# Sliding-window attention with a soft mixture of experts: long q and k runs with 32x32 vector transposes, one span of keys per query tile, dilated heads by residue, experts on four array columns

## The chip, the core and the metric

The kernel runs on one core of one Trainium2 chip. The metric is the device time of one execution in microseconds (us), here always the median of several executions. A kernel that is compared was run on the same chip, in turn with the kernel before. Runs more than 1.5% above the fastest run of the same kernel count as slow and are left out of every ratio.

In the profile, PE is TensorE's matmuls, PEld its loads of stationary operands, DVE is VectorE, ACT is ScalarE and POOL is GpSimd. GpSimd issues all large loads and stores here. "GB/s" counts bytes as they land in the on-chip memory. The inputs are fp32 in HBM and land as fp16, so a landed rate of 207 GB/s reads about twice as much from HBM; the outputs land as fp32.

## The reference

There are two stages in series. Attention has batch 8, 8 heads, 576 positions and 64 elements per head. Heads 0-3 ("plain") look back over 32 positions; heads 4-7 ("dilated") look back over 128 positions but only at every fourth.

```
scores = q @ k.T / sqrt(64)
rel = pos_q - pos_k
plain: 0 <= rel < 32          dilated: 0 <= rel < 128 and rel % 4 == 0
x = softmax(where(mask, scores, -1e9)) @ v      # then heads side by side: [4608, 512]

logits = x @ phi                                # [4608, 32], 8 experts x 4 slots
d = softmax(logits, over rows); c = softmax(logits, over slots)
slot_in = d.T @ x                               # [32, 512]: needs ALL rows of x
slot_out[e] = relu(slot_in[e] @ w1[e]) @ w2[e]  # w1: 512x1024, w2: 1024x512, per expert
out = c @ slot_out                              # [4608, 512]
```

The experts can start only when attention is finished for all rows, and no output row exists before the last expert's second layer. So the time is a sum of three stages: attention, experts, output.

q and k are drawn with a standard deviation of 0.1. A scaled score is therefore about 0.01 in size, and the softmax is nearly uniform over the window. The comparison with the reference cannot see an error in the scores.

## The kernel before

Loads go through GpSimd's queue, in blocks of 128 positions. Every row that lands is 64 elements: 256 bytes are read, 128 bytes land. A memset of the column of ones (which gives the softmax sum as a 65th output) stands behind each v load.

```
def load_qk_blk(ti, b, blk):
    ...
    src = ten[b, :, s0 : s0 + ns, :].rearrange("h p d -> p h d")
    nc.gpsimd.dma_start(out=t[0:ns], in_=src)

def load_v_blk(b, kb):
    ...
    nc.gpsimd.dma_start(
        out=vt[0:nk, :, 0:D], in_=v[b, :, s0 : s0 + nk, :].rearrange("h p d -> p h d")
    )
    nc.gpsimd.memset(vt[0:nk, :, D : D + 1], 1.0)
```

TensorE transposes q and k, two heads at a time, and VectorE copies each result out of PSUM. Scores are then one matmul per head and key block, on 64 rows of the array.

```
# transposes of one tensor and one pair of heads: 5 matmuls, then one copy
nc.tensor.transpose(ring[:, blk, 0:ns], inp, ident16[0:ns, 0:ns])
...
nc.vector.tensor_copy(out=tt, in_=ring.rearrange("r b c -> r (b c)")[:, 0:S])
...
for h in range(2):                       # emit_scores
    p0 = 64 * h
    nc.tensor.matmul(sps[0:nk, h, 0:ncol], kT[p0 : p0 + 64, q0 : q0 + nk],
                     qT[p0 : p0 + 64, q0 : q0 + ncol], start=True, stop=True)
```

The experts run one after another. Each matmul has only the 4 slots of one expert as its stationary operand, and 512 moving columns.

```
for fc in range(2):                      # emit_expert_w1(e)
    hps = psum_h.tile([S_PER_E, 512], FP32, ...)
    for dc in range(4):
        nc.tensor.matmul(hps, siT[:, dc, 4 * e : 4 * e + 4],
                         w1t[:, dc, 512 * fc : 512 * fc + 512], ...)
...
for hc in range(FDIM // 128):            # emit_expert_w2(e)
    nc.tensor.matmul(sops, hT_sb[:, hc, :], w2t[:, hc, :], start=(hc == 0), stop=(hc == 7))
```

The loads of batch b+1 are issued while batch b computes. Five w1/w2 pairs are loaded during attention, the other three after it.

The softmax here doesn't subtract the row's maximum and nothing guards it: scores larger than these inputs give would overflow.

## Time and profile before

The time before was 291.85 us (median of 3, 287.37 to 293.52). One profiled execution had a span of 287.0 us.

| stage | from, to (us) | what limits it |
|---|---|---|
| attention, 8 batches | 0-213 | loads, with TensorE close behind |
| experts, 128 matmuls | 213-258 | matmuls in series, late weight loads |
| output, 9.4 MB | 260-287 | DMA, up to 407 GB/s |

These are lines of the page of the kernel before: busy time per engine, then the span in 40 equal slices (a digit is the busy share in tenths), the landed rate in each slice, and the count of DMA packets by size.

```profile
span 287.0 us, 4940 instructions
...
PE 243.9 (85%) x1786; PEld 123.8 (43%) x1786; DVE 142.9 (50%) x478; ACT 113.6 (40%) x318; POOL 139.9 (49%) x220
...
PE   5469799895899979987998799689996999969990
...
DMA  9999999999999999999999999900009999408999
GB/s 116 127 96 126 82 115 124 153 175 115 114 174 176 102 112 193 166 114 116 190 150 111 135 186 136 111 5 2 0 3 177 204 208 210 83 2 232 407 405 275
DMA packets 131208, 41.09 MB, mean 143 GB/s; under 512 B 114128, under 2 KB 122352, under 8 KB 131184
```

The DMA row stands at 9 up to the 26th slice (187 us), but the rate below it wanders between 82 and 193 GB/s, while the weights that are loaded late move at 204-210. 114,128 of the 131,208 packets are below 512 B. So the DMA engines are busy with short rows. TensorE is busy for 85% of the span.

The timeline of GpSimd in the kernel before shows the issues (start, duration, line, operation, and in brackets the idle time before it and what ended that):

```profile
56.06 0.88 POOL L134 DMA_DIRECT2D v_0_974<-in_v_dram  x1 [1.21 <-PE s_2_4_903 L200]
56.93 0.89 POOL L127 DMA_DIRECT2D qk_3_1_1015<-in_q_dram  x1
57.79 0.90 POOL L127 DMA_DIRECT2D qk_3_1_1017<-in_k_dram  x1
58.95 0.89 POOL L134 DMA_DIRECT2D v_1_1019<-in_v_dram  x1 [0.26 <-issue]
68.16 0.13 POOL L137 MEMSET v_0_974<- 128x8 f16 x1 [8.31 <-DMA v_0_974<-in_v_dram]
```

Each issue costs 0.9 us, and there are 15 per batch. The memset behind the load of v block 0 waits for that load to land, and everything behind it in GpSimd's queue waits too: 8.3 us here. The view of waits of the same kernel has one such line per batch:

```profile
POOL v_0_2177 L137 <- DMA v_0_2177<-in_v_dram: 10.0, 1, 10.0
POOL v_0_1375 L137 <- DMA v_0_1375<-in_v_dram: 9.6, 1, 9.6
```

The chain of waits that ended last confirms it. From 56 us on, its long pieces are (start, duration, piece):

```profile
56.06 12.05 DMA v_0_974<-in_v_dram
...
82.31 13.11 DMA v_0_1375<-in_v_dram
```

The two stand 26 us apart, which is the time of one batch. How close TensorE follows is seen in two windows of the kernel before: one batch in the middle, and the last batch, for which nothing is loaded any more. Columns: window, length, busy time of PE, PEld, DVE, ACT, POOL, granted clock, the time that DMA packets took as a share of the 16 engines' time (above 1 where they overlap), GB/s.

```profile
56.00:82.00 26.00, 21.41 (x202) 12.60 (x202) 16.03 (x61) 10.95 (x37) 14.39 (x22) 0.71 1.54 140
187.00:209.00 22.00, 21.21 (x160) 11.54 (x160) 13.48 (x45) 10.88 (x42) 0.13 (x1) 0.58 0.00 1
```

Without loads the last batch takes about 22 us instead of 26, with TensorE busy for 21.2 of them. So mending the loads alone could not give more than some 5 us per batch; TensorE's work has to shrink as well.

### The profile page before, as it was taken

How to read it: one execution, taken by the hardware profiler on the slowest of the kernel's cores; microseconds unless marked ns; L12 is line 12 of the kernel's file. 1: busy time of each engine (PE TensorE's matmuls, PEld its weight loads, DVE VectorE, ACT ScalarE, POOL GpSimd, SP SyncE). 2: the span in 40 equal slices, each digit the busy share in tenths (PEclk: the TensorE clock that was granted, in tenths of full speed). 3: DMA queues.
4: the chain of work that ended last, by engine and by line, in shares of the span. 5: the costliest groups of instructions: out<-in, count | busy, mean ns of one | idle time of the engine just before them, and what ended most of it. 6: DMA issues, size and time to landing. Idle time of an engine off the chain costs nothing.

```text
span 287.0 us, 4940 instructions
## 1 busy us (share of the span) xinstructions
PE 243.9 (85%) x1786; PEld 123.8 (43%) x1786; DVE 142.9 (50%) x478; ACT 113.6 (40%) x318; POOL 139.9 (49%) x220
## 2 busy tenths in 40 slices
PE   5469799895899979987998799689996999969990
PEld 1135455553446544554455446436552343322110
DVE  2038566867266764765466448636763000006662
ACT  1015443643434434362344235333713344426551
POOL 7888587634780658087419634600012110007993
PEclk9855555979555675595566557755789799995555
DMA  9999999999999999999999999900009999408999
GB/s 116 127 96 126 82 115 124 153 175 115 114 174 176 102 112 193 166 114 116 190 150 111 135 186 136 111 5 2 0 3 177 204 208 210 83 2 232 407 405 275
DMA packets 131208, 41.09 MB, mean 143 GB/s; under 512 B 114128, under 2 KB 122352, under 8 KB 131184
## 3 DMA queue, kind: packets, MB, share of 16 engines
q0 software_dynamic: 130304, 40.38, 125.4%
q1 hardware_dynamic: 880, 0.39, 0.7%
q8 instruction: 14, 0.23, 0.4%
q14 instruction: 10, 0.08, 0.1%
HBM read 62.23 MB, written 9.44 MB: 250 GB/s over the span
## 4 chain that ended last, share of the span: by engine, by line
DMA 41%; PE 29%; POOL 16%; issue 8%; ACT 2%; DVE 1%; POOLq 0%; ACTq 0%
POOL out_dram L575 5%; DMA v_0_2177<-in_v_dram 5%; DMA v_0_1375<-in_v_dram 5%; DMA v_0_974<-in_v_dram 4%; DMA v_0_2578<-in_v_dram 4%; DMA v_0_1776<-in_v_dram 4%; DMA v_2_208<-in_v_dram 2%; DMA v_2_2664<-in_v_dram 2%; DMA v_3_1913<-in_v_dram 2%; DMA v_3_1111<-in_v_dram 2%; DMA v_2_1461<-in_v_dram 2%; DMA v_0_159<-in_v_dram 2%; DMA v_3_180<-in_v_dram 2%; DMA v_0_194<-in_v_dram 2%; DMA qk_6_4_2349<-in_k_dram 2%
## 5 line engine op out<-in xcount | busy, mean ns | idle before, releaser
L575 POOL DMA_DIRECT2D out_dram<-outt_3702 x1 | 0.6, 561 | 28.2 <-ACT outt_3702 L564 28.2
L148 POOL DMA_DIRECT2D w_5_3378<-in_moe_w_dram x1 | 0.8, 766 | 25.9 <-PE o_2_4_3291 L256 25.9
L561 PEld LDWEIGHTS <-ET 32*128 32x128 f16 (+1 forms) x40 | 4.2, 116 | 19.7 <-issue 19.5
L388 PE MATMUL warm_136<-masks_sb 128*128 128x512 f16 x16 | 6.4, 591 | 3.4 <-DMA masks_sb<-masks_d 3.4
L510 PEld LDWEIGHTS <-siT 128*4 128x4 f16 x64 | 5.2, 90 | 8.4 <-issue 2.4
L350 PEld LDWEIGHTS <-E_row 128*32 128x32 f16 (+1 forms) x40 | 4.1, 114 | 9.8 <-issue 8.7
L310 PEld LDWEIGHTS <-phi_64 128*32 128x32 f16 x64 | 5.5, 109 | 5.4 <-issue 3.9
L213 ACT ACTIVATE praw_0_0_271<-s_0_0_257 128x318 f16<-128x318 f32 x1 | 0.4, 438 | 17.2 <-PE s_0_0_257 L200 17.2
L388 PEld LDWEIGHTS <-masks_sb 128*128 128x128 f16 x30 | 3.2, 121 | 7.8 <-issue 4.1
L256 PEld LDWEIGHTS <-ptm_76 128*128 128x128 f16 (+1 forms) x64 | 4.9, 113 | 3.6 <-issue 0.9
L173 DVE COPY qT_0_225<-ring_q_0_226 128x576 f16<-128x576 f16 x1 | 0.5, 458 | 11.7 <-PE ring_q_1_234 L169 11.7
L256 PEld LDWEIGHTS <-ptm_82 128*128 128x128 f16 (+1 forms) x64 | 5.0, 117 | 3.0 <-issue 0.6
L256 PEld LDWEIGHTS <-ptm_85 128*128 128x128 f16 (+1 forms) x64 | 5.5, 119 | 0.8
L256 PEld LDWEIGHTS <-ptm_79 128*128 128x128 f16 (+1 forms) x64 | 4.9, 118 | 1.5 <-issue 0.7
L330 PEld LDWEIGHTS <-ET 32*128 32x128 f16 (+1 forms) x40 | 3.7, 100 | 3.7 <-issue 1.2
L148 POOL DMA_DIRECT2D w_7_3423<-in_moe_w_dram x1 | 0.8, 759 | 8.8 <-PE hps_1_3417 L510 8.8
L137 POOL MEMSET v_0_2177<- 128x8 f16 x1 | 0.1, 133 | 10.0 <-DMA v_0_2177<-in_v_dram 10.0
L137 POOL MEMSET v_0_1375<- 128x8 f16 x1 | 0.1, 133 | 9.6 <-DMA v_0_1375<-in_v_dram 9.6
L256 PEld LDWEIGHTS <-ptm_83 128*128 128x128 f16 (+1 forms) x48 | 3.7, 118 | 2.4 <-DVE qT_1_832 L173 0.6
L256 PEld LDWEIGHTS <-ptm_77 128*128 128x128 f16 (+1 forms) x48 | 3.7, 117 | 2.3 <-issue 0.9
L256 PEld LDWEIGHTS <-ptm_80 128*128 128x128 f16 (+1 forms) x48 | 3.8, 117 | 1.3
L137 POOL MEMSET v_0_2578<- 128x8 f16 x1 | 0.1, 133 | 8.4 <-DMA v_0_2578<-in_v_dram 8.4
(2096 smaller groups left out, 879.8 us busy)
## 6 DMA issues: line engine op xcount, KB each, us to landing
w_0_860<-in_moe_w_dram POOLq DMA_DIRECT2D x1, 1024.0 KB, 8.3
w_0_862<-in_moe_w_dram POOLq DMA_DIRECT2D x1, 1024.0 KB, 12.9
w_1_1261<-in_moe_w_dram POOLq DMA_DIRECT2D x1, 1024.0 KB, 8.1
w_1_1263<-in_moe_w_dram POOLq DMA_DIRECT2D x1, 1024.0 KB, 11.9
w_2_1662<-in_moe_w_dram POOLq DMA_DIRECT2D x1, 1024.0 KB, 8.1
w_2_1664<-in_moe_w_dram POOLq DMA_DIRECT2D x1, 1024.0 KB, 11.5
w_3_2063<-in_moe_w_dram POOLq DMA_DIRECT2D x1, 1024.0 KB, 8.1
w_3_2065<-in_moe_w_dram POOLq DMA_DIRECT2D x1, 1024.0 KB, 13.3
```

What stands on the lines that cost most here:

```text
L137: nc.gpsimd.memset(vt[0:nk, :, D : D + 1], 1.0)
L148: nc.gpsimd.dma_start(out=w1t, in_=moe_w1[e].rearrange("(c p) f -> p c f", p=128))
L173: nc.vector.tensor_copy(out=tt, in_=ring.rearrange("r b c -> r (b c)")[:, 0:S])
L213: nc.scalar.activation(out=praw[0:nk, :, 0:ncol], in_=sps[0:nk, :, 0:ncol], func=AF.Exp, scale=SCALE)
L256: nc.tensor.matmul(opair[0:nq, col, :], lhs, rhs, start=(i_mm == 0), stop=(i_mm == len(mms) - 1),)
L310: nc.tensor.matmul(lp[:, 0:ncl], phi16[:, kc, :], xTb[:, kc, c0 : c0 + ncl], start=(kc == 0), stop=(kc == 3),)
L330: nc.tensor.transpose(erps[0:ns], ET_sb[:, r0 : r0 + ns], ident16[0:32, 0:32])
L350: nc.tensor.matmul(up, E_row[0:ns, blk, :], xb[0:ns, t, :], start=(iu == 0), stop=(iu == NQB - 1),)
L388: nc.tensor.matmul(wps, lhs, rhs, start=True, stop=True)
L510: nc.tensor.matmul(hps, siT[:, dc, 4 * e : 4 * e + 4], w1t[:, dc, 512 * fc : 512 * fc + 512], start=(dc == 0), stop=(dc == 3),)
L561: nc.tensor.matmul(fp[0:ns], ET_sb[:, r0 : r0 + ns], so_sb, start=True, stop=True)
L575: nc.gpsimd.dma_start(out=out[r0 : r0 + ns, :], in_=ot[0:ns])
```

## The change

Four things are rewritten at once. The intent is to make rows long and take transposes off TensorE, to cut the matmul columns that the mask throws away, and to run four experts side by side.

1. **Loads.** One q or k load brings 4 heads x 576 positions as 128 partitions of 18 positions each: runs of 4608 bytes read, 2304 landed. Dilated v comes in runs of four positions and is spread by GpSimd. Plain v still comes in 64-element rows, in six loads of 96 positions, each with its four heads. The columns of ones are written once, at the start.
2. **Transposes.** VectorE transposes q and k in 32x32 blocks of 4-byte words (two fp16 each), 6 instructions per batch.
3. **Scores.** A plain query tile of 96 positions meets one span of 128 keys. Dilated heads are sorted by position modulo 4, so that each residue is an ordinary window of 32. Scores contract over 32 rows twice.
4. **Experts.** Four experts write to four 32-column groups of the array.

The diff, cut to its core ("..." marks cuts):

```diff
-        src = ten[b, :, s0 : s0 + ns, :].rearrange("h p d -> p h d")
-        nc.gpsimd.dma_start(out=t[0:ns], in_=src)
...
+            nc.gpsimd.dma_start(
+                out=t, in_=ten[b].rearrange("(g h) (p j) d -> (h p) g (j d)", g=2, j=PJ)
+            )
...
+    def load_v_plain(b):
+        vt = vP[b % NV]
+        for t in range(NT):
+            nc.gpsimd.dma_start(
+                out=vt[32:128, t, :, 0:D],
+                in_=v[b, 0:4, QT * t : QT * t + QT, :].rearrange("h a d -> a h d"),
+            )
...
+        nc.gpsimd.dma_start(
+            out=sa, in_=v[b, 4:8, 0:512, :].rearrange("h (a r) d -> a h (r d)", r=DIL)
+        )
+        nc.gpsimd.dma_start(
+            out=sb[0:48], in_=v[b, 4:8, 384:576, :].rearrange("h (a r) d -> a h (r d)", r=DIL)
+        )
...
-            nc.vector.tensor_copy(out=tt, in_=ring.rearrange("r b c -> r (b c)")[:, 0:S])
+        src = raw[(ti, b)][:, 0, :].bitcast(U32).rearrange("p (j m) -> p j m", m=32)
+        t = qTp[b % 2] if ti == 0 else kTp[b % 2][:, 32 : 32 + S, :]
+        dst = t.rearrange("p s t -> p (s t)").bitcast(U32).rearrange("p (a j) -> p j a", j=PJ)
+        nc.vector.transpose(out=dst, in_=src)
...
+        for kt_, k0, qt_, q0, c0, w in jobs:
+            for tt in range(2):
+                for hh in range(2):
+                    p0 = 32 * (2 * pair + hh)
+                    nc.tensor.matmul(
+                        sps[:, hh, c0 : c0 + w],
+                        kt_[p0 : p0 + 32, k0 : k0 + 128, tt],
+                        qt_[p0 : p0 + 32, q0 : q0 + w, tt],
+                        start=(tt == 0),
+                        stop=(tt == 1),
+                    )
...
+            if att and kt == 1:
+                if b + 2 < B:
+                    load_qk(0, b + 2)
+                    load_qk(1, b + 2)
+                    load_w1(b)
...
+            if att and kt == 3 and b + 2 < B:
+                load_v_plain(b + 2)
+                load_v_dil(b + 2)
...
+    for fc in range(2):
+        for g in range(2):
+            for dc in range(4):
+                for j in range(4):
+                    e = 4 * g + j
+                    nc.tensor.matmul(
+                        hps[32 * j : 32 * j + 32, fc, :],
+                        siTm[:, dc, e, :],
+                        w1t[e][:, dc, 512 * fc : 512 * fc + 512],
...
+    jobs = [(0, c, j) for c in range(8) for j in range(4)]
+    jobs += [(1, c, j) for j in range(4) for c in range(8)]
+    for g, c, j in jobs:
+        nc.tensor.matmul(
+            so[32 * j : 32 * j + 32, :],
...
```

## The prediction

> **What bounds the kernel now.** Three stages in series (table of windows).
> Attention, 0-213 us. The 40-slice view shows the DMA engines at 9 tenths from 0 to 187 us but only 82-193 GB/s landed (fp16, half of what is read), while the late weight loads land 204-210. 114,128 of 131,208 packets are under 512 B (queue line): q, k and v come as 256-byte rows. The chain of waits between 56 and 187 us is mostly loads of 11-13 us with GpSimd issues of 0.9 us each; a memset behind each v load makes the GpSimd queue wait 8-10 us per batch (view of waits). A batch takes 26 us. TensorE is close behind: once everything has landed (187-209 us) the last batch still takes about 21 us, at a granted clock of 0.5-0.8, about 110 ns for each of its 190 matmuls.
> Experts, 213-258 us: 128 matmuls of 512 columns with 4 stationary columns, about 240 ns apart, in series.
> Output, 258-287 us: 9.4 MB at up to 407 GB/s, DMA-bound.
>
> **What the change does.**
> 1. q and k rows become 2304-byte landed runs, half of v 512-byte; only half of v keeps 128-byte landed rows. All loads are 62 MB read. At the 410 GB/s read that the late weight loads show, plus some 8 us for the short v rows (20 ns per row and engine, from the first two batches: 27,648 rows in 35 us), that is an estimate of 160 us for all loads, 15 us per batch with one w1 each. The memsets behind loads go.
> 2. The q/k transposes (320 matmuls, 64 PSUM copies of 0.38 us) leave TensorE; VectorE gets 6 transposes per batch, about 0.35-0.65 us each at one element per cycle (estimate from its 0.33 us per 256 fp32 elements).
> 3. Scores: 112 small matmuls per batch instead of 40, on 32 rows. Matmuls per batch rise from 190 to 240, but columns fall from 24,000 to 19,000. Estimate at the half clock, from the trace's 69 ns per 65-column attention-value matmul and 0.83 ns per column: scores 6-7, values 4, x transposes 2, logits 2, E rows and U 2.5 us, plus drains: 18-19 us per batch. Trainium skill, "TensorEngine Tiling (Array Packing)", Key Properties: changing the tiling mode drains TensorE; the new order mixes 32-row and full-row work, and no trace here shows the price. VectorE: about 11.5 us, ScalarE 7.5 us, GpSimd 11 us per batch: not limiting.
> 4. Experts four abreast: "TensorE: Matmul & The Clock Gate", Part 3, gives 3.07x for four row tiles and 2.38x for three column tiles; not shown here. The first layer should fall from 15 to about 5 us; of the second, half is issued one expert after another and keeps 240 ns per matmul (about 8 us).
>
> **Sum.** Start 10 us; eight batches x 18.5 = 148 (TensorE-bound now, DMA just below it); from the last scores to the first output 27 us (before, 45): back end 11, experts 14, issue 2; output 25. Total about 210 us. The floor, if TensorE were quicker, is loads 160 + 5 + 26 = 191.
>
> Predicted 208 us, range 191 to 226. Chances: faster 0.97, same 0.02, slower 0.01.
>
> **What would show each step.** Right: packets fall to about 40,000; landed rate near 200 GB/s when DMA is busy; batches 17-20 us apart; chain in attention through TensorE, not loads; experts' first layer under 6 us; output unchanged at 25 us.
> Wrong: batches near 15 us (scores overlap on row groups, warm clock); batches above 21 us (drains, or VectorE or GpSimd in the chain); GpSimd's v copies above 3 us each, delaying issues; the last w2 loads landing after the hidden layer, making the second layer wait on DMA.

## The result, and the profile after

The changed kernel took 210.70 us (median of 4 runs, 208.66 to 212.04) against 291.53 us for the kernel before in the same rounds (287.37 to 293.52). The ratio is 0.726, with a 95% interval of 0.717 to 0.735: faster by 27%. A ratio is the mean time of one kernel's fast runs over the mean of the other's of the same rounds, so it is not quite the ratio of the medians.

The profiled run of that set was its slowest (212.04 us, marked slow because it lies over 1.5% above the fastest). The lines below are therefore from a repeat of the same kernel, called a_same in the experiments, whose profiled run was fast: 210.64 us, span 208.9 us. First the page, as above, with its line for the chain of waits:

```profile
span 208.9 us, 5183 instructions
...
PE 150.2 (72%) x2128; PEld 93.2 (45%) x2128; DVE 132.3 (63%) x346; ACT 84.1 (40%) x134; POOL 105.7 (51%) x156
...
PE   0124578969789899899899899987579765756700
...
DMA  6999999999999999999999999999999995499992
GB/s 119 158 174 201 122 202 211 146 195 212 124 149 211 182 157 212 184 155 212 186 137 210 187 157 202 195 206 207 207 207 207 207 206 94 116 407 404 407 408 73
DMA packets 48057, 41.54 MB, mean 199 GB/s; under 512 B 21281, under 2 KB 35233, under 8 KB 48033
...
PE 40%; issue 23%; DMA 11%; DVE 8%; ACT 8%; POOL 6%; POOLq 0%; DVEq 0%
```

Packets are down to 48,057 and TensorE's busy time from 243.9 to 150.2 us. The mean rate is 199 GB/s. But the rate dips in about every third slice, that is every 16 us: 122, 146, 124, 157, 155, 137. The chain gives TensorE 40% and DMA only 11%, which seems to say that TensorE sets the pace. That reading is tested below, and for the total it does not hold.

Two windows of the kernel after: one batch, and the stretch from the last scores to the first expert layer. Columns as before.

```profile
72.00:88.00 16.00, 14.77 (x241) 10.22 (x240) 13.38 (x38) 8.57 (x15) 9.47 (x13) 0.50 1.27 184
...
134.50:155.00 20.50, 14.31 (x213) 10.26 (x212) 9.78 (x32) 7.95 (x15) 3.25 (x4) 0.50 1.24 207
```

No engine is busy for the whole 16 us. TensorE has 14.77 and VectorE 13.38 us of work; the rate is 184 GB/s, below the 207 of the second window. A batch has two rhythms, and they have to be told apart. Its loads: GpSimd issues the q loads 16.4 us apart (39.56 to 105.28 us). Its computing: VectorE's q transposes start 16.5 us apart (50.21 to 116.32 us).

GpSimd's timeline for one batch of the kernel after:

```profile
58.79 0.75 POOL L175 DMA_DIRECT2D w<-in_moe_w_dram  x1
59.52 1.06 POOL L166 COPY vD<-vsa 128x1024 f16<-128x1024 f16 x1
60.50 1.33 POOL L166 COPY vL<-vsb 48x1024 f16<-48x1024 f16 x1
61.79 3.98 POOL L147 DMA_DIRECT2D vP<-in_v_dram  x6
66.46 0.75 POOL L156 DMA_DIRECT2D vsa<-in_v_dram  x1 [0.69 <-DMA raw<-in_k_dram]
72.46 0.58 POOL L159 DMA_DIRECT2D vsb<-in_v_dram  x1 [5.25 <-DMA vP<-in_v_dram]
73.03 0.71 POOL L134 DMA_DIRECT2D raw<-in_q_dram  x1
```

Between the load of v for dilated heads (vsa, 66.46) and its small rest (vsb, 72.46) GpSimd waits 5.25 us. Every later load stands behind vsb. The view of waits sums it (total, times, longest):

```profile
POOL vsb L159 <- DMA vP<-in_v_dram: 25.0, 5, 5.6
...
POOL w L181 <- PE o L292: 16.5, 1, 16.5
```

The profile names the plain v load as the releaser, since it came last by its record. The landing times say otherwise. The built program gives the loads that GpSimd issues one of eight semaphores in turn, so a load is issued only when the one eight places earlier has landed. A batch has 11 loads (q, k, w1, six of plain v, vsa, vsb), and vsb is the eighth after w1, which is the 1 MB load. w1 landed at 38.44, 55.31, 71.90 and 87.67 us; vsb was issued at 38.99, 55.87, 72.46 and 88.23 us, always 0.55 or 0.56 us later. When w1 has landed, only six 48 KB pieces and the 256 KB of vsa remain under way: 544 KB, 2.7 us of data at 207 GB/s. The stream runs thin each time.

The experts, on TensorE's timeline of the kernel after (hps is the first layer, so the second):

```profile
155.01 6.43 PE L547 MATMUL hps<-w,siTm 128*32 128x512 f16 x64 [0.62 <-DVE siTm L533]
...
163.84 6.19 PE L581 MATMUL so<-w,hTm 128*32 128x512 f16 x48 [0.52 <-DVE hTm L570]
171.75 1.89 PE L581 MATMUL so<-w,hTm 128*32 128x512 f16 x8 [1.71 <-DMA w<-in_moe_w_dram]
174.29 1.02 PE L581 MATMUL so<-w,hTm 128*32 128x512 f16 x4 [0.65 <-DMA w<-in_moe_w_dram]
176.83 1.02 PE L581 MATMUL so<-w,hTm 128*32 128x512 f16 x4 [1.51 <-DMA w<-in_moe_w_dram]
```

The first layer takes 6.43 us for 64 matmuls; the kernel before had TensorE busy for 17.61 us with its 64. The second layer waits three times for w2 (1.71, 0.65 and 1.51 us). (GpSimd's 16.5 us in the view above is the wait of late w2 loads for memory that attention still holds. Loads issued before it kept landing until 161.64 us, and the next landed at 166.68, so it cost no supply here.) The last piece of w2 landed at 176.78 us, the first output was issued 3.4 us later, at 180.16 us, and the output took the remaining 28.7 us. So the span is the sum: last weight landed (176.8), 3.4, output (28.7). The end of attention, at 134.5 us, is not a term of it.

### The profile page after: what moved, and what is told of

Same layout as the page of the kernel before. It is cut to its first block, busy times and chain, and to the rows that moved or that the text cites. A ratio compares the mean times of both kernels' runs of the same rounds, so it can differ in the third digit from the quotient of the medians.

```text
span 210.3 us, 5183 instructions
## 1 busy us (share of the span) xinstructions
PE 151.5 (72%) x2128; PEld 92.8 (44%) x2128; DVE 134.4 (64%) x346; ACT 84.2 (40%) x134; POOL 105.7 (50%) x156
## 4 chain that ended last, share of the span: by engine, by line
PE 36%; issue 23%; DVE 13%; DMA 10%; ACT 8%; POOL 7%; POOLq 0%; DVEq 0%
DMA raw_1_172<-in_k_dram 6%; POOL out_dram L605 3%; DMA raw_0_135<-in_k_dram 3%; ACT ET L351 2%; DMA out_dram<-ot_3287 2%; DVE vP_98 L172 1%; DVE kTd_92 L197 1%; DVE pd_5_2443 L244 1%; POOL w_7_3029 L181 1%; DVE pd_5_1034 L244 1%; PE s_4_2038 L226 1%; DVE vP_99 L172 1%; DVE qTd_96 L197 1%; PE s_5_2771 L226 1%; DVE kTp_89 L188 1%
## 5 line engine op out<-in xcount | busy, mean ns | idle before, releaser
L226 PEld LDWEIGHTS <-kTp_89 32*128 32x128 f16 x192 | 6.7, 121 | 14.4 <-DVE kTp_89 L188 10.4
L147 POOL DMA_DIRECT2D vP_98<-in_v_dram x18 | 12.2, 685 | 1.3 <-DMA vsa_165<-in_v_dram 1.1
L348 PEld LDWEIGHTS <-phi_61 128*128 128x128 f16 x64 | 7.8, 131 | 9.7 <-issue 5.6
L147 POOL DMA_DIRECT2D vP_97<-in_v_dram x18 | 12.0, 678 | 0.0
L226 PEld LDWEIGHTS <-kTd_91 32*128 32x128 f16 x256 | 7.2, 112 | 7.4 <-DVE emask L436 3.7
L597 PEld LDWEIGHTS <-ET 128*128 128x128 f16 x36 | 3.6, 99 | 15.4 <-issue 14.1
L226 PEld LDWEIGHTS <-kTd_92 32*128 32x128 f16 x256 | 7.6, 111 | 4.3 <-issue 2.0
L226 PEld LDWEIGHTS <-kTp_90 32*128 32x128 f16 x192 | 6.9, 122 | 5.6 <-DVE kTp_90 L188 1.8
L181 POOL DMA_DIRECT2D w_5_3025<-in_moe_w_dram x1 | 0.9, 881 | 15.6 <-PE o_10_2919 L292 15.6
L147 POOL DMA_DIRECT2D vP_99<-in_v_dram x12 | 8.0, 677 | 0.0
L581 PEld LDWEIGHTS <-hTm_3042 128*32 128x32 f16 x32 | 3.0, 103 | 9.8 <-issue 7.4
L588 ACT CAST so_sb<-so 128x256 f16<-128x256 f32 x1 | 0.4, 372 | 14.3 <-PE so L581 14.3
L581 PE MATMUL so<-w_6_3027,hTm_3042 128*32 128x512 f16 x8 | 2.5, 467 | 3.1 <-DMA w_6_3027<-in_moe_w_dram 3.1
L362 PEld LDWEIGHTS <-ET 32*128 32x128 f16 x48 | 1.9, 101 | 5.5 <-ACT ET L351 5.5
L393 PEld LDWEIGHTS <-ones 96*128 96x128 f16 x48 | 4.0, 104 | 0.0
L188 DVE STREAM_TRANSPOSE qTp_93<-raw_0_133 128x576 uint32<-128x576 uint32 x1 | 1.3, 1260 | 4.1 <-DMA raw_0_133<-in_q_dram 4.1
## 6 DMA issues: line engine op xcount, KB each, us to landing
w_7_83<-in_moe_w_dram POOLq DMA_DIRECT2D x1, 1024.0 KB, 13.4
```

Source lines behind the costliest of these rows:

```text
L147: nc.gpsimd.dma_start(out=vt[32:128, t, :, 0:D], in_=v[b, 0:4, QT * t : QT * t + QT, :].rearrange("h a d -> a h d"),)
L188: nc.vector.transpose(out=dst, in_=src)
L226: nc.tensor.matmul(sps[:, hh, c0 : c0 + w], kt_[p0 : p0 + 32, k0 : k0 + 128, tt], qt_[p0 : p0 + 32, q0 : q0 + w, tt], start=(tt == 0), sto ...
L348: nc.tensor.matmul(lp, phi4[:, kc].rearrange("p c s -> p (c s)"), rhs, start=(kc == 0), stop=(kc == 3))
L393: nc.tensor.matmul(up[:, c, :], l, rr, start=(i == 0), stop=(i == len(jobs) - 1), skip_group_check=True)
L581: nc.tensor.matmul(so[32 * j : 32 * j + 32, :], hTm[g][:, c, 32 * j : 32 * j + 32], w2t[4 * g + j][:, c, :], start=(g == 0 and c == 0), st ...
```

## The experiments

Theory 1 is the supply of loads: the stream of loads sets the time, and the wait of vsb behind w1 makes it slower than it needs to be (1a in later expectations). Its rivals are that TensorE sets the batch time, as predicted and as the chain suggests, and that VectorE does, with masks and transposes. They are called the TensorE and the VectorE theory below; the expectations say what each stands for in a run. All ratios below are to the kernel before of the same rounds, whose medians were 287.21 us in the first set, 290.02 in the second and 288.61 in the third. Each set ran on another chip, so versions of different sets are compared by their ratios, and a difference of a few us between their times is rough. Medians and ranges are of all runs, slow ones included.

### a_same: the kernel after, unchanged

> The changed kernel again, unaltered, as the yardstick for the next three on the same chip. All theories: 208 to 212 us, batches about 16.3 us apart.

Measured: 210.72 us (210.44 to 213.13), ratio 0.739 (0.732 to 0.746), correct. It is the yardstick of the first set.

### a_vp_head: plain v in four loads, one per head, instead of six

```diff
-        for t in range(NT):
+        for h in range(4):
             nc.gpsimd.dma_start(
-                out=vt[32:128, t, :, 0:D],
-                in_=v[b, 0:4, QT * t : QT * t + QT, :].rearrange("h a d -> a h d"),
+                out=vt[32:128, :, h, 0:D],
+                in_=v[b, h].rearrange("(t a) d -> a t d", a=QT),
             )
```

> The plain v load of a batch as four DMAs (one per head) instead of six (one per tile); same bytes, same 256-byte rows, correct result. Theory 1 (supply: GpSimd stalls about 4.7 us per batch before the last v load, until the w1 load eight DMAs back has landed, and the DMA queue meanwhile runs low): that wait falls below 2 us, the batches come 14.5 to 15.5 us apart, and the total falls by 6 to 12 us, to 198 to 204 us. Theory 2 (TensorE-bound, as predicted) and theory 3 (VectorE-bound): period and total unchanged within 2 us.

Measured: 195.63 us (195.51 to 195.72), ratio 0.684 (0.680 to 0.688), correct. That is 15 us less than a_same, more than expected. The same rows and bytes are moved (47,799 packets against 48,057), and the compute is untouched. Its page, and GpSimd's timeline for one batch:

```profile
GB/s 114 171 193 207 186 212 207 187 212 203 190 213 203 191 212 203 192 211 201 192 214 198 194 211 209 208 207 208 207 206 207 210 194 40 202 408 407 408 408 118
DMA packets 47799, 41.52 MB, mean 214 GB/s; under 512 B 21024, under 2 KB 34976, under 8 KB 47776
```

```profile
59.68 0.59 POOL L159 DMA_DIRECT2D vsb<-in_v_dram  x1
60.25 0.72 POOL L134 DMA_DIRECT2D raw<-in_q_dram  x1
65.22 0.72 POOL L134 DMA_DIRECT2D raw<-in_k_dram  x1 [4.25 <-DVE xd L303]
```

There are nine loads per batch now, and vsb goes out with no wait. The eighth load after w1 is the next k. It does wait (4.25 us): w1 landed at 64.68 us and k was issued at 65.22, again 0.54 us later. But q, vsa, vsb and the plain v, 1216 KB, are under way meanwhile, over twice as much as before. The dips shrink to 184-193 GB/s, the loads of a batch are issued 14.3 us apart (q, 18.43 to 89.79 us) instead of 16.4, and the last w2 lands at 162.83 instead of 176.78 us. The first output follows 3.4 us later, as before. This is what the supply theory asks for. It also shows that the short rows of plain v alone don't explain the 16.4 us, since they are as many and as short as they were.

The computing of a batch did not come down to 14.3 us. Between the q transposes of two batches, first a_same, then a_vp_head, columns as before:

```profile
67.42:83.52 16.10, 14.87 (x242) 10.22 (x240) 13.48 (x39) 8.67 (x15) 9.27 (x13) 0.50 1.26 184
...
80.82:96.63 15.81, 14.59 (x242) 10.29 (x240) 13.61 (x38) 8.66 (x15) 8.74 (x12) 0.50 1.32 203
```

Four batches of a_vp_head in a row took 15.8 us each (16.5 on average in a_same), and neither trace shows TensorE, VectorE or ScalarE waiting for a load between 48 and 116 us. So the loads now run ahead of the computing, and the last scores end at 130.6 us, only 3.9 us earlier than in a_same. Of the 14.0 us by which the first output comes earlier, 7.6 lie in the second expert layer, which took 14.0 us in a_same and takes 6.4 here, where w2 is nearly in time. The rest lies before it, and why the computing became 0.7 us per batch quicker is not shown.

### a_half_scores: only one of the two halves of every score contraction (deliberately wrong)

```diff
-            for tt in range(2):
+            for tt in range(1):
...
-                        start=(tt == 0),
-                        stop=(tt == 1),
+                        start=True,
+                        stop=True,
```

> Wrong result on purpose: only the first of the two 32-deep halves of each score product, so 56 score matmuls per batch instead of 112. Theory 2: about 2.5 to 3 us of TensorE per batch go, so the period falls from 16.3 to about 13.5 us and the total by about 10 us or more. Theory 1 and 3: period 16 us or a little under, total within 3 us of the unaltered kernel.

Measured: 209.17 us (206.81 to 210.12), ratio 0.729 (0.720 to 0.737). The intervals of a_same and this run overlap. It was reported correct: the scores are too small for the comparison to see. One batch of this kernel, columns as before:

```profile
72.86:88.94 16.08, 11.98 (x185) 7.66 (x184) 13.43 (x38) 8.43 (x14) 10.26 (x14) 0.66 1.27 185
```

TensorE lost 2.8 us of work per batch (11.98 against 14.77), and the batch still takes 16.1 us. The chain of waits now names VectorE where it named TensorE in a_same:

```profile
issue 25%; DVE 24%; PE 22%; DMA 12%; ACT 7%; POOL 6%; POOLq 0%; DVEq 0%; ACTq 0%
```

The two engines are close enough that either can hold a batch near 16 us, so an unchanged batch time alone does not clear both. The end of attention decides: the last scores end at 127.6 us instead of 134.5, 6.9 us earlier, yet the last w2 lands at 175.95 us (176.78 in a_same) and the first output is issued at 179.75 us (180.16). The time did not follow TensorE's work in attention. As an account of the total, the TensorE theory falls.

### a_no_mask: the mask multiplies left out (deliberately wrong)

```diff
-            if 0 <= pb < B:
+            if 0 <= pb < 0:
                 emit_mask(pb, pk)
```

> Wrong result on purpose: the six mask multiplications of a batch are left out, about 2.9 us of VectorE. Theory 3: period about 13.5 us and total about 10 us or more below the unaltered kernel. Theory 1 and 2: within 3 us of it.

Measured: 210.50 us (209.15 to 212.72), ratio 0.739 (0.731 to 0.747). The result was wrong (relative error 0.40). One batch:

```profile
72.72:88.48 15.76, 13.14 (x225) 9.80 (x226) 10.01 (x30) 8.94 (x14) 9.45 (x14) 1.00 1.31 190
```

VectorE went from 13.4 to 10.0 us per batch, and the time did not move. The VectorE theory falls. (Work was taken from one engine at a time; no run takes it from both.) Taking work from either engine changes the total by no more than the noise, and rearranging loads changes 15 us: the stream of loads, up to the last w2, sets the time.

### a_interleave: the same 11 loads per batch in another order

```diff
                 if b + 2 < B:
+                    load_v_plain(b + 2, (0, 1, 2))
                     load_qk(0, b + 2)
+                    load_v_plain(b + 2, (3, 4))
+                    load_w1(b)
                     load_qk(1, b + 2)
-                    load_w1(b)
+                    load_v_plain(b + 2, (5,))
+                    load_v_dil(b + 2)
...
-            if att and kt == 3 and b + 2 < B:
-                load_v_plain(b + 2)
-                load_v_dil(b + 2)
```

> The changed kernel, correct, with the same eleven loads per batch in another order and all asked for at one place: three v pieces, q, two v pieces, w1, k, one v piece, then the two dilated v loads. Number, sizes and GpSimd's issue time unchanged. Theory 1a (a load waits until the one eight before it has landed, so a row of small loads leaves little in flight; here every row of eight holds a large load): the batches come 14.3 to 15.5 us apart, total 195 to 203 us. Theory 1b (six short v loads cost more than four in GpSimd time or in the DMA engines): total 206 us or more.

Measured: 204.70 us (203.65 to 205.22), ratio 0.709 (0.704 to 0.715), correct. The loads did as the supply theory says: q loads at 40.13, 54.68, 69.04, 84.19 and 98.77 us, so 14.7 us apart on average, still with six pieces of plain v. So the same eleven loads, in another order and asked for at one place, recover most of the loads' period, and GpSimd's time for two more issues is not what held a_same back. But the total missed the expected range. The last w2 landed at 170.23 us, and two losses can be seen. The slices of the first 30 us went as low as 150 and 84 GB/s. And the computing did not follow the loads: from 53.66 to 120.04 us its batches stood 16.6 us apart, and the last scores ended at 140.1 us, later than in a_same (134.5). The mask multiplies on VectorE took 4.6 us per batch there against 3.6. Neither the cause of that nor the share of each loss is shown.

### b_long_qk: the kernel before, q and k read as long runs (deliberately wrong order of positions)

```diff
-        src = ten[b, :, s0 : s0 + ns, :].rearrange("h p d -> p h d")
-        nc.gpsimd.dma_start(out=t[0:ns], in_=src)
+        flat = ten[b].rearrange("h s d -> (h s d)")
+        src = flat[512 * s0 : 512 * (s0 + ns)].rearrange("(p x) -> p x", x=512)
+        nc.gpsimd.dma_start(out=t[0:ns].rearrange("p h d -> p (h d)"), in_=src)
```

> The kernel before, with one edit that makes the result wrong on purpose: each partition of a q or k load reads one contiguous 2 KB run (1 KB landed) instead of eight 256-byte rows; bytes, number of loads and all compute stay. If the short rows bound the kernel before: batches fall from 26 us towards the 21 us that the last batch took without loads, total 255 to 272 us. If TensorE bounds it: within 4 us of before. If the memset behind each v load bounds it: also little, under 6 us.

Measured: 263.85 us (262.70 to 270.44, the last a slow run), ratio 0.912 (0.903 to 0.922). It was reported correct although the scores are wrong, as above. Packets fell to 66,696. So long rows alone, with all compute as it was, are worth 26 us.

### b_memset_first: the kernel before, with each memset ahead of its load

```diff
+        nc.gpsimd.memset(vt[0:nk, :, D : D + 1], 1.0)
         nc.gpsimd.dma_start(
             out=vt[0:nk, :, 0:D], in_=v[b, :, s0 : s0 + nk, :].rearrange("h p d -> p h d")
         )
-        nc.gpsimd.memset(vt[0:nk, :, D : D + 1], 1.0)
```

> The kernel before, correct, with the memset of the ones column issued ahead of the v load instead of behind it, so that GpSimd does not wait for the load to land. If GpSimd's wait is what held the loads: the 8 to 10 us waits per batch go, total 265 to 280 us. If the rate of short rows or TensorE is the bound: within 4 us of before.

Measured: 268.54 us (267.01 to 275.46), ratio 0.925 (0.913 to 0.938), correct. Two of the five runs were slow (274 and 275 us). Moving one line is worth 21 us.

### b_both: the two together

The edit is the sum of the last two.

> Both edits of the kernel before together (wrong result on purpose). If loads bound its attention stage and TensorE is close behind at about 21 us per batch: 245 to 262 us, and not lower, since transposes, experts and output are as before.

Measured: 256.43 us (254.00 to 258.99), ratio 0.885 (0.874 to 0.896). The two gains do not add up (26 + 21 would be 47; it is 34), because TensorE stands behind them. One batch of this kernel:

```profile
60.00:81.00 21.00, 20.64 (x184) 11.90 (x182) 13.98 (x51) 10.19 (x34) 9.51 (x18) 0.65 1.30 174
```

TensorE is busy for 20.64 of 21 us. Here the batch is bound by TensorE. So these two edits of the loads give 34 of the 80 us with the old compute. The other 46 us came only with the rest of the change, the new compute above all; no run splits them fully.

### a_serial_experts: the kernel after, experts issued one after another

```diff
-            for dc in range(4):
-                for j in range(4):
+            for j in range(4):
+                for dc in range(4):
                     e = 4 * g + j
...
-    jobs = [(0, c, j) for c in range(8) for j in range(4)]
+    jobs = [(0, c, j) for j in range(4) for c in range(8)]
```

> The changed kernel, correct, with the experts' matmuls issued one expert after another in both layers, so that no two neighbours use different array columns. If the four-abreast order matters and is not hidden by waiting for the last weights: the first layer grows from 5.8 us to about 14 us, the first half of the second from 1.8 us to about 7 us, total up by 7 to 13 us. If the last weight loads (landing 176 us) hide it: up by less than 3 us.

Measured: 210.66 us (209.21 to 212.04), ratio 0.729 (0.722 to 0.737), correct. The time did not change, and at first this looked like "the experts are hidden behind the w2 loads". TensorE's timeline of this kernel shows that the edit did not do what it was meant to do:

```profile
156.37 5.04 PE L547 MATMUL hps<-w,siTm 128*32 128x512 f16 x64 [0.62 <-DVE siTm L533]
...
163.84 6.30 PE L581 MATMUL so<-w,hTm 128*32 128x512 f16 x48 [0.52 <-DVE hTm L570]
```

The first layer took 5.04 us, 79 ns per matmul. In the built program the order was as edited: four matmuls of expert 0, four of expert 1, and so on. In the trace the first four start at 156.369, 156.383, 156.400 and 156.413 us, and the next four 0.4 us later. On one column group, four matmuls in a row start 0.4 us apart at this point and 0.215 us apart later (next experiment). So the four that start together are one of each expert: TensorE started matmuls of other column groups ahead of earlier-issued ones of the same group. The waits in the records settle it. The matmuls that wait for w1 of experts 5, 6 and 7 stand at places 21, 25 and 29 of the program; they are the 18th, 19th and 20th to start (158.063, 158.082 and 158.095 us). The experts were still abreast, and as a test of what that is worth this run is inconclusive.

### a_one_column: all experts on the same 32 columns (deliberately wrong)

```diff
-                        hps[32 * j : 32 * j + 32, fc, :],
+                        hps[0:32, fc, :],
...
-            so[32 * j : 32 * j + 32, :],
+            so[0:32, :],
```

The two PSUM tiles are also zeroed first, and the start and stop flags are set for one group.

> Wrong result on purpose: all experts write the same 32 partitions, so they share one group of array columns; order and number of matmuls unchanged. If the four column groups are what makes the experts quick and this is not hidden by the last weight loads: first layer 14 to 20 us instead of 5.8, the first half of the second 6.9 us instead of 1.8, total 216 to 224 us. If hidden by the last loads: within 3 us of 210.7.

Measured: 222.36 us (221.49 to 222.78), ratio 0.771 (0.767 to 0.776), wrong (relative error 1.45). TensorE's timeline:

```profile
157.31 16.04 PE L548 MATMUL hps<-w,siTm 128*32 128x512 f16 x64 [0.62 <-DVE siTm L533]
...
175.73 13.99 PE L583 MATMUL so<-w,hTm 128*32 128x512 f16 x64 [0.52 <-DVE hTm L571]
```

The first layer takes 16.04 us instead of 6.43, with matmuls 0.43 us apart at first and 0.215 us later; the second takes 13.99 us with no wait for w2. The last w2 landed at 177.59 us, as in a_same, but the first output was issued only at 192.03 us. So four column groups are worth some 12 us in the time of the kernel after (11.7 between medians of two sets, 11.9 between the first outputs of the two profiled runs); the rest of what they save is hidden behind the w2 loads. The edit also makes all matmuls add to the same rows of PSUM, which this run cannot tell from the shared columns. The pace says more than the totals. In a_same, four matmuls start within 10 ns, and the fours start 0.42 us apart for most of the stage and 0.215 at its end; on one column, single matmuls start 0.43 and then 0.215 us apart. So four abreast took the time of one.

### best1: a_vp_head, and the overlapping part of dilated v copied on chip instead of loaded

```diff
         nc.gpsimd.dma_start(
-            out=sb[0:48], in_=v[b, 4:8, 384:576, :].rearrange("h (a r) d -> a h (r d)", r=DIL)
+            out=sb[32:48], in_=v[b, 4:8, 512:576, :].rearrange("h (a r) d -> a h (r d)", r=DIL)
         )
...
+        nc.vector.tensor_copy(
+            out=vL[b % NV][0:32, :, :, 0:D], in_=sa[96:128].rearrange("a h (r d) -> a h r d", r=DIL)
+        )
```

> Correct. The four-piece v load, and the 128 dilated rows per head that were read twice are copied on the chip by VectorE instead: 1.05 MB less read, 2.6 us at 410 GB/s. If the loads still bound the kernel up to the first output: 192 to 194 us. If VectorE (12 of 14.3 us busy per batch) has become the bound: 195 us or more.

Measured: 196.29 us (195.73 to 198.18), ratio 0.683 (0.677 to 0.688), correct. Not faster than a_vp_head. There is 0.5 MB less to load, but VectorE has one more copy, and the loads of a batch are issued 15.05 us apart instead of 14.3, because q now waits up to 3.3 us for VectorE. The computing of a batch takes 16.0 us (50.84 to 114.81 us), with VectorE busy for 14.5 of them. The tail of the loads shows where time was lost: a late w2 load was issued at 143.36 us, when attention had freed its memory (140.91 in a_vp_head), and landed 8.1 us after the one before it, where about 5 is usual; the last w2 landed at 165.84 us (162.83). So the next saving has to come from the computing of attention as well as from the loads. No run tests that.

### best2: best1, with the loads spread between q, w1 and k

The edit orders the loads of a batch as plain v head 0, q, head 1, w1, head 2, k, head 3, then dilated v, all at the earlier place in the loop.

> Correct. As best1, and the loads of a batch interleaved, small between large, so that the DMA queue should never run low. If a little supply is still lost per batch: 189 to 192 us. If the queue is already full all the time: as best1 within 1.5 us.

Measured: 200.85 us (198.08 to 201.34), ratio 0.694 (0.687 to 0.701), correct, and slower than best1. The view of waits names a new one:

```profile
POOL vP L147 <- PE o L264: 19.7, 5, 7.1
```

Issued earlier, the first plain v load has to wait until TensorE has finished with the buffer it writes to, 19.7 us in all, and the loads behind it wait as well.

The best version is a_vp_head at 195.6 us, 7% below the kernel after and 32% below the kernel before. By their ratios (0.684 and 0.683) best1 cannot be told from it.

## Why the prediction was right, and where it was not

**The time.** 208 us was predicted, 210.7 measured, inside the range of 191 to 226. Part of that is luck: two terms of the sum were wrong in opposite directions.

| term of the sum | predicted | a_same |
|---|---|---|
| start and eight batches, to the last scores | 158 | about 134.5 |
| last scores to first output | 27 | 45.6 |
| output | 25 | 28.7 |
| sum | 210 | 208.9 (span) |

**The step that failed.** It is this one: "eight batches x 18.5 = 148 (TensorE-bound now, DMA just below it)". Two things in it failed. The first is its size: the computing of a batch took 16.5 us in a_same and 15.8 us in a_vp_head, with TensorE busy for 14.6 to 15.0, so TensorE's work was put too high (17-20 us was to show it right). That TensorE stands in the chain of attention was right, but VectorE stands so close that 2.8 us less of TensorE's work left the batch near 16 us. The second is the path: the sum runs from the end of attention through the experts to the output, and the first output did not wait for that. In a_half_scores attention was over 6.9 us earlier, and the first output moved by 0.4 us. In its place stands the stream of loads, from the first load to the last w2 at 176.8 us. The estimate of 160 us for all loads was not wrong as a floor: a_vp_head had them all in at 162.8 us. What was missing is the stall in the queue (25.0 us of waiting in five batches), whose removal took 15 us off the total. The prediction did not look at how many loads the program lets be under way.

**The stretch before the output.** "From the last scores to the first output 27 us": 45.6 us in a_same. Two of its terms were off. The back end, from the last scores to the first expert layer, took 20.5 us (predicted 11). It took 18.9 us in a_vp_head too, so this is not the loads: the term was mis-sized, and no run says which part of it. The experts took 22.8 us (predicted 14), but 14.4 us in a_vp_head, where w2 was there nearly in time. So nearly all of that excess is the late loads again: 3.9 us of plain waits, and matmuls that go a few at a time as the pieces land. The prediction had listed "the last w2 loads landing after the hidden layer" among what would show it wrong, and that is what happened. The output took 28.7 us instead of 25.

**Loads.** Long rows as the main cost of the kernel before: shown by b_long_qk (26 us) and, for the memset, by b_memset_first (21 us). The landed rate near 200 GB/s: 199. Packets: 48,057 against "about 40,000".

**Compute.** That TensorE's work had to shrink as well: shown by b_both, which stops at 256 us with TensorE full. The transposes on VectorE took twice the estimate (1.24 us for 576 words against 0.35-0.65), and VectorE had 13.4 us per batch instead of 11.5:

```profile
L188 DVE STREAM_TRANSPOSE qTp<-raw x8: 1228/1246/1256, 6.7 to 116.3; 128x576 uint32<-128x576 uint32 x8
L188 DVE STREAM_TRANSPOSE kTp<-raw x8: 1224/1244/1259, 8.3 to 119.6; 128x576 uint32<-128x576 uint32 x8
```

(The columns are minimum, median and maximum duration in ns, first and last start, forms.) In total it did no harm that the runs show (3.4 us less work on VectorE per batch, in a_no_mask, gained nothing), though in attention VectorE stands close behind TensorE. The Trainium skill, "Vector Engine (DVE) Microarchitecture Reference", section 3.8, says that a transpose sustains one element per cycle per lane. Here the shortest form of these transposes, 256 words, took 0.62 us (median) and the 576-word form 1.245, so 2.0 ns per further word; nothing here separates the operation from its strided output.

**Experts.** "From 15 to about 5 us" for the first layer: 6.43 us, and 16.04 us on one column. Four abreast is shown, by 2.5 times in total, and by four times where the pace is the same (fours as far apart as single matmuls on one column). The Trainium skill, "TensorE: Matmul & The Clock Gate", Part 3, "Measured speedup vs the span model", gives 2.38 times for three column tiles and no figure for four.

**Clock and drains.** The feared drain at a change of tiling ("TensorEngine Tiling (Array Packing)", Key Properties) remains open as a size: no run isolates one. The computing of a whole batch, drains and all, took 15.8 us in a_vp_head, against the 18-19 us of an estimate that included them. The granted clock in the records does not explain times here: two fast runs of the kernel after with mean clocks of 0.949 and 0.666 took 209.68 and 208.66 us, and in a_one_column the records grant 1.00 through the whole first layer while its matmuls went from 0.43 to 0.215 us apart. The Trainium skill warns in "TensorE: Matmul & The Clock Gate", Part 1, "Seeing it yourself", that such clock events have been seen to be unreliable, and this agrees.

## What to carry to other kernels

Count the loads that are under way, not only their bytes: if the program reuses a fixed number of semaphores, one large load holds back the load that many places behind it, and a row of small loads between the two leaves too few bytes in flight. Fewer, larger small loads around a big one were worth 15 us here, with the same bytes and rows. When the chain of waits names an engine, take some of that engine's work away before believing it: the chain said TensorE 40%, and with less work on TensorE attention ended 6.9 us earlier but the output only 0.4. When two engines are nearly full, look at what the end of the stage moves, not at the batch time alone: the second engine holds the batch when the first is relieved. Follow the last load that the serial tail needs (here the last w2): it plus the tail gave the time in a_same and in a_vp_head.

## What the Trainium skill lacked or had wrong

- "DMA: Bandwidth & Descriptors", section "Why a DMA increments its semaphore by 16 and not by 1", asks for one semaphore per transfer in flight, but neither it nor the other sections draw the consequence for speed: with eight semaphores in turn, a load was issued 0.54 to 0.56 us after the one eight places earlier had landed, and the loads of a batch came 16.4 us apart where they came 14.3 apart with less waiting (210.7 against 195.6 us in total).
- "TensorE: Matmul & The Clock Gate", Part 3, "The mechanism", says that matmuls are strictly first in, first out, without reordering. In a_serial_experts, issued four in a row per column group, matmuls of four column groups started within 44 ns of each other, and 64 of them took 5.04 us (79 ns each), where one column group spaces them by 215 ns at its quickest. The matmuls at places 21, 25 and 29 of the program were the 18th, 19th and 20th to start. The order of starts across column groups was not the order of issue.
- The same page, "Measured speedup vs the span model", has three column tiles (2.38 times) but not four: 16.04 us on one column against 6.43 us on four (5.04 us with the experts issued in a row), for 64 matmuls of 512 columns. These totals mix two paces; at the slower, fours started 0.42 us apart and single matmuls on one column 0.43, so four took the time of one.
- No page has a duration for a transpose of 4-byte words with a strided output (it would belong to "Vector Engine (DVE) Microarchitecture Reference", section 3.8): 128x576 words took 1.24 us, 2.0 ns per further word.
